# The MLP's input features in another order: weights loaded to match, four heads' worth of copies made whole, one pair of heads moved by DMA

## The chip, the cores and the metric

The kernel runs on one core of a Trainium2 chip. Its engines are TensorE (PE: matmuls, with weight loads PEld), VectorE (DVE), ScalarE (ACT), GpSimd (POOL) and SyncE (SP, which issues DMAs). The metric is the device time of one execution in microseconds. Before the change it is 640.87 us, the median of three runs (640.73 to 641.13).

## The reference

Two stages. The first is a delta-rule recurrence over 768 tokens for 4 batches and 8 heads of size 48; its output, with the heads side by side, is the input of an MLP with 384 inputs, 2048 hidden units and SiLU.

```python
B, H, S, D = q.shape                      # 4, 8, 768, 48
k_n = k / (norm(k) + 1e-6)
for t in range(S):
    y[t] = q[t] @ state
    state = state + beta[t] * outer(k_n[t], v[t] - k_n[t] @ state)
x = y.transpose(0, 2, 1, 3).reshape(B * S, H * D)   # 3072 x 384
h = x @ w_in                              # 384 x 2048
out = (h / (1 + exp(-h))) @ w_out         # 2048 x 384
```

The weights arrive as 64-bit floating point numbers. The kernel reads them as pairs of 32-bit words and makes fp32 of them itself.

## The kernel before

**Attention.** The 768 tokens are six chunks of 128, a chunk c is two halves hf of 64. Inside a chunk the recurrence is solved as a triangular system: scores of keys with keys, an inverse of blocks of 32x32 (`invert`, on VectorE: for each m one L628 and one L633), a merge of blocks (`merge`, L783; for the first chunk `merge_half`, L807), then `keys`, `inner`, `update` of the state, and the outputs: `old` (L909, queries with the state) and `new` (L922, scores with the new values), both into a PSUM bank pyc. The four batches are two groups g of two. Heads come in NP = 4 pairs p with members e. In pyc a head (p, e) takes the 48 rows from 64 * (1 - e) and the columns of p: the odd heads are at rows 0 to 47, the even ones at rows 64 to 111.

**From attention to the MLP.** A half-chunk's MLP input is the tile xT: 128 partitions, NKT = 3 tiles of 128 features, 256 tokens (64 of each batch). Feature f = 48 * head + d is at partition f % 128 of tile f // 128, so heads cross partitions and tiles. `even_heads` copies the odd heads' 48 rows of pyc into the tile part in one copy (48x512), and the even heads into xT in six copies of 48, 32 or 16 rows. Both are by ScalarE (L545) or, once, by VectorE (L548). The odd heads then go from part to xT by DMA, five for a half-chunk, issued by SP in `move` (L902). Matmuls of the first MLP layer (`hidden`, L1049, into the PSUM tile phid) read xT; ScalarE's SiLU is L1059. For the first half of chunk 0 there is no state yet, and `first_outputs` (L887) multiplies straight from a copy of the new values in the tile slab (which lies in sums_of_w) into two banks, one for even and one for odd heads; xT is the first (L545) with the second added (L896).

**Weights.** w_in is fetched in eight pieces of 256 columns, each by three DMAs of 128 partitions (`fetch_w_in`, L292), into whatever room is free then: tiles named raw, w_out or sums_of_g in the profile. `narrow` turns a piece into fp32 in steps: two activations on ScalarE (L232, L233), two operations on VectorE (L237, L241), one on GpSimd (L245). Pieces 0 to 7 are narrowed in order. w_out follows in eight pieces (L306).

**What sets the order.** Every engine's instructions are pinned to the order in which the code emits them. Around the change it is written out by hand, in a string of letters (`script`): r runs half a step of the MLP, f and b push a weight piece on (f its next step, b its beginning), i a step of `invert` of chunk 1, p a step of `prepare(1)`, s one of `solve`. All of SP's DMAs are one line (`in_line`), issued in order. Where `deep` is set, a DMA also waits until the one two places before it in the line has landed. That is so for the loads of q of chunk 1 and for fetches 3, 6 and 5; fetches 0, 1, 2 and 4 are issued without it. Their order on SP is: k and q of chunk 0; fetches 0 and 1; k of chunk 1; v of chunk 0; fetch 2; q of chunk 1; fetches 4, 3, 6 and 5; fetch 7. Then, around 95 us, `block_in` (L583) reads the 32x32 blocks of chunk 1 back from DRAM into g, the factors that `invert` starts from, and the first `move` follows it.

For chunk 1, `invert` ends in `put_up`: two block transposes (L606 into xe_y, which the merges read as a moving operand, and L608 into up) and copies.

Of the kernel before, what the change touches and what calls it, by code (L numbers as in the profile page):

```python
# [19 lines left out]
def kernel(  # L20
# [13 lines left out]
    P = 128  # L34
# [236 lines left out]
    SLAB = B * NP * 2 * D + D  # L271
# [10 lines left out]
    def fetch_w_in(i):  # L282
# [7 lines left out]
        src = moe_w_in.rearrange("(a p) f -> p a f", p=P)[:, :, i * WF : (i + 1) * WF].bitcast(U32)  # L290
        for a in range(NKT):
            in_line(nc.sync.dma_start(out=raw[:, a], in_=src[:, a]))  # L292
# [309 lines left out]
    def put_up(x):  # L602

        both = work.tile([P, BH, T], FP32, name="xe_y", tag="g", bufs=1)
        xes[1], ys[1] = both[:], both[:].rearrange("p (g h) t -> p g h t", g=2)
        pin(nc.vector.transpose(out=both[:].rearrange("p n s -> p s n"), in_=x))  # L606
# [229 lines left out]
    def inner(c, g, hf, room=CC):  # L836
# [9 lines left out]
        if c == 0 and hf == 0:  # L846
            by = (by_act, by_dve) if g == 0 else (by_dve, by_act)
            at = slab[:, g * HB * NP * 2 * D + D :][:, 0 : HB * NP * 2 * D]
# [27 lines left out]
    def first_outputs(g):  # L876

        pys = [bank(A, f"py{e}") for e in range(2)]
        for u in range(HB):
            for a in range(NKT):  # L880
                for n in range(2):
                    for half in range(2):
                        f = P * a + W * half
                        h = f // D + n
                        p, e = h // 2, h % 2
                        at = ((g * HB + u) * NP + p) * 2 * D + D + f - D * h
                        pin(nc.tensor.matmul(  # L887
                            pys[e][HALVES[half], C * a + W * u : C * a + W * (u + 1)],
                            lhsT=slab[on(e, 0, g), at : at + W], rhs=aps[0, g][1][on(e, 0, g), u, h, :],
                            start=True, stop=True,  # L890
                        ))
        xT, half = x_half(0, g, 0)
        to = xT[:, :, half]
        even, odd = (py[:, 0 : NKT * C].rearrange("p (a t) -> p a t", a=NKT) for py in pys)
        by_act(to, even)
        pin(nc.vector.tensor_tensor(out=to, in0=to, in1=odd, op=ALU.add))  # L896
# [20 lines left out]
    def new(c, g, hf):  # L917
# [8 lines left out]
        copies.append(even_heads(c, g, hf, py))  # L926
# [4 lines left out]
    def even_heads(c, g, hf, py):  # L931

        xT, half = x_half(c, g, hf)
        if g == 0:
            parts[c, hf] = work.tile([P, 2, NP, C], FP32, name="part", tag="x", bufs=1)
        part = parts[c, hf][:, g]
        by = by_dve if c == 1 and hf == 0 and g == 1 else by_act
        by(part[0:D], py[0:D].rearrange("p (a t) -> p a t", a=NP))
        if c == 0:
            yield  # L940
        for h in chained(range(1, H, 2), range(0, H, 2)):
            if c > 0 and h == 0:
                yield
            f = D * h
            while f < D * (h + 1):
                n, at = min(D * (h + 1) - f, P - f % P), W * (1 - h % 2) + f - D * h
                while h % 2 == 0 and (n > T and at % W or f % P % W and n > T):
                    n = T
                to = xT[f % P : f % P + n, f // P, half]
                if h % 2 == 1:  # L950
                    if g == 1:
                        moves.append((
                            xT[f % P : f % P + n, f // P].rearrange("p (g t) -> p g t", g=2),
                            parts[c, hf][at : at + n, :, h // 2, :],
                        ))
                else:
                    by(to, py[at : at + n, C * (h // 2) : C * (h // 2 + 1)])
# [655 lines left out]
```

## Time and profile before

| | |
|---|---|
| median of three runs | 640.87 us |
| profiled execution | 646.08 us, its span 644.3 us |
| granted TensorE clock, mean | 0.973 |
| TensorE busy | 623.5 us, 97% |
| VectorE, ScalarE, GpSimd busy | 401.2, 217.2, 94.3 us |
| moved by DMA | 53.69 MB |

The profile is of one execution of its own, longer than the timed ones. It gives each instruction by engine and line of the kernel, with its output and inputs (out<-in), and, behind a number in brackets or a bar, the idle time of the engine before it and what ended that. A row of the view by stage gives the stretch, its length, busy time and number of instructions of PE, PEld, DVE, ACT and POOL, then the granted TensorE clock, the share of time in which the DMA engines were busy, and GB/s. A row of waits gives who waited, for whom, the sum in us, how often, and the longest. The chain of waits is followed back from the last instruction; a row has its start, its length and what it was. In the timeline a row has start, length, engine, line and instruction; SPq is the issuing of a DMA by SP, waits included where rows are merged. A row of DMA issues ends with KB each and the median us from issue to landing. Rows by tile give minimum, median and maximum in ns.

### The profile page before, as it was taken

How to read it: one execution, taken by the hardware profiler on the slowest of the kernel's cores; microseconds unless marked ns; L12 is line 12 of the kernel's file. 1: busy time of each engine (PE TensorE's matmuls, PEld its weight loads, DVE VectorE, ACT ScalarE, POOL GpSimd, SP SyncE). 2: the span in 40 equal slices, each digit the busy share in tenths (PEclk: the TensorE clock that was granted, in tenths of full speed). 3: DMA queues.
4: the chain of work that ended last, by engine and by line, in shares of the span. 5: the costliest groups of instructions: out<-in, count | busy, mean ns of one | idle time of the engine just before them, and what ended most of it. 6: DMA issues, size and time to landing. Idle time of an engine off the chain costs nothing.

```text
span 644.3 us, 21893 instructions
## 1 busy us (share of the span) xinstructions
PE 623.5 (97%) x9642; PEld 550.1 (85%) x9642; DVE 401.2 (62%) x917; ACT 217.2 (34%) x512; POOL 94.3 (15%) x96
## 2 busy tenths in 40 slices
PE   6879999999999999999999999999999999999997
PEld 4677787756789988999989989989989989889997
DVE  5845688988865986563987563987464974212112
ACT  2655656151342122451122451122451122441120
POOL 5332630237011020010020010020001000000000
PEclk9759799999999999999999999999999999999999
DMA  9755445170278433268434268334173033100101
GB/s 190 164 141 163 146 97 132 50 148 3 58 150 145 62 85 50 54 133 136 70 79 55 47 137 138 69 79 56 26 154 76 9 79 48 40 14 1 25 0 25
DMA packets 141695, 53.69 MB, mean 83 GB/s; under 512 B 113296, under 2 KB 135056, under 8 KB 141600
## 3 DMA queue, kind: packets, MB, share of 16 engines
q1 hardware_dynamic: 141264, 52.14, 40.2%
q8 instruction: 76, 1.25, 0.8%
q10 hardware_dynamic: 336, 0.15, 0.1%
q14 instruction: 19, 0.16, 0.1%
HBM read 39.62 MB, written 10.49 MB: 78 GB/s over the span
## 4 chain that ended last, share of the span: by engine, by line
PE 92%; DMA 2%; issue 2%; DVE 1%; ACT 1%; SPq 1%; POOL 0%; DVEq 0%; POOLq 0%
PE phid L1049 39%; PE px L1156 16%; PE py L1156 12%; PE po L1084 7%; PE pa L530 3%; PE pz L841 2%; PE ph L829 2%; PE pyc L922 2%; PE pu L861 2%; PE pyc L909 2%; PE pt L501 1%; DMA kb<-in_k_dram 1%; DMA xT<-part 1%; PE px L783 1%; PE py L783 1%
## 5 line engine op out<-in xcount | busy, mean ns | idle before, releaser
L1049 PE MATMUL phid<-xT,w_in 128*128 128x256 f32 x1152 | 259.6, 383 | 2.5 <-DMA xT<-part 1.5
L1049 PEld LDWEIGHTS phid<-xT,w_in 128*128 128x128 f32 x1152 | 217.2, 191 | 33.6 <-issue 4.1
L1059 ACT ACTIVATE gT<-phid 128x512 f32<-128x512 f32 x88 | 52.6, 598 | 147.1 <-PE phid L1049 138.5
L628 DVE SCALAR_TENSOR_TENSOR rank<-g,step,x 128x31 f32<-128x31 f32 (+15 forms) x124 | 49.7, 401 | 36.9 <-DMA g<-blocks 33.4
L1138 DVE TENSOR_TENSOR sums_of_g<-gT 128x384 f32<-128x384 f32 (+1 forms) x60 | 29.8, 516 | 56.5 <-ACT gT L1059 46.0
L1156 PE MATMUL py<-w_out,sums_of_g 128*128 128x192 f32 x320 | 56.8, 329 | 0.0
L1156 PE MATMUL px<-sums_of_w,sums_of_g 128*128 128x192 f32 x320 | 56.6, 329 | 0.0
L1156 PEld LDWEIGHTS px<-sums_of_w,sums_of_g 128*128 128x128 f32 x320 | 52.2, 190 | 0.5
L1156 PEld LDWEIGHTS py<-w_out,sums_of_g 128*128 128x128 f32 x320 | 52.2, 190 | 0.4
L633 DVE TENSOR_TENSOR x<-x,rank 128x31 f32<-128x31 f32 (+15 forms) x124 | 42.5, 343 | 4.3
L468 POOL TENSOR_TENSOR vf<-vf,n_slot 128x768 f32<-128x768 f32 x10 | 14.9, 1490 | 167.9 <-DMA vf<-in_v_dram 121.8
L868 DVE TENSOR_TENSOR state<-state,pu 48x384 f32<-48x384 f32 x44 | 24.3, 552 | 21.9 <-PE pu L861 20.9
L545 ACT COPY xT<-pyc 48x128 f32<-48x128 f32 (+2 forms) x126 | 32.7, 260 | 1.7
L489 DVE STREAM_TRANSPOSE kq<-stage 128x512 f32<-128x512 f32 x28 | 28.2, 1112 | 3.9 <-DMA stage<-in_q_dram 3.8
L1156 PE MATMUL px<-sums_of_w,gT 128*128 128x192 f32 x160 | 28.4, 329 | 0.0
L1156 PE MATMUL py<-w_out,gT 128*128 128x192 f32 x160 | 28.4, 329 | 0.0
L1156 PE MATMUL px<-w_out,gT 128*128 128x192 f32 x160 | 28.0, 327 | 0.0
L841 PEld LDWEIGHTS pz<-vf,xi 64*64 64x64 f32 x768 | 25.2, 142 | 3.2 <-issue 2.6
L551 POOL COPY g<-x 64x256 f32<-64x256 f32 x4 | 5.0, 1242 | 152.5 <-DVE x L636 152.5
L1156 PEld LDWEIGHTS px<-w_out,gT 128*128 128x128 f32 x160 | 26.4, 190 | 0.6
L841 PE MATMUL pz<-vf,xi 64*64 64x48 f32 x768 | 26.9, 226 | 0.0
L1156 PEld LDWEIGHTS py<-w_out,gT 128*128 128x128 f32 x160 | 26.1, 190 | 0.3
(197 smaller groups left out, 831.1 us busy)
## 6 DMA issues: line engine op xcount, KB each, us to landing
vf<-in_v_dram SPq DMA_DIRECT2D x48, 96.0 KB, 3.1
out_dram<-o SPq DMA_DIRECT2D x42, 96.0 KB, 2.2
w_out<-in_moe_w_in_dram SPq DMA_DIRECT2D x12, 256.0 KB, 3.5
sums_of_w<-in_moe_w_out_dram SPq DMA_DIRECT2D x8, 384.0 KB, 4.4
blocks<-ap SPq DMA_DIRECT2D x40, 64.0 KB, 1.9
g<-blocks SPq DMA_DIRECT2D x5, 512.0 KB, 3.7
kb<-in_k_dram SPq DMA_DIRECT2D x12, 192.0 KB, 4.4
kb<-in_k_dram SPq DMA_DIRECT2D x24, 96.0 KB, 4.5
```

The lines of the kernel that those rows point to most:

```text
L489: pin(nc.vector.transpose(out=kqs[c, b][:, :, j, :].rearrange("p a (i m) -> p a m i", i=T), in_=src.rearrange("p a (m d) -> p a m d", d=D) ...
L530: pin(nc.tensor.matmul(pa[e][half, p * n * W : (p + 1) * n * W], lhsT=kq[rows, p, 0, half], rhs=kq[rows, p, js[0] : js[-1] + 1, half], sta ...
L545: return pin(nc.scalar.copy(to, of))
L628: pin(nc.vector.scalar_tensor_tensor(out=tv, in0=g[:, 0:m, m : m + 1].to_broadcast([P, m, n]), scalar=step[:, m : m + 1], in1=x[:, m : m + ...
L633: yield pin(nc.vector.tensor_tensor(out=x[:, 0:m, m:T], in0=x[:, 0:m, m:T], in1=tv, op=ALU.add))
L841: yield pin(nc.tensor.matmul(pz[rows, n * D : (n + 1) * D], lhsT=xis[g][rows, u * H + 2 * p + e, :], rhs=vfs[c][rows, hf, g * HB + u, p, : ...
L868: pin(nc.vector.tensor_tensor(out=to, in0=to, in1=by_heads(pu[of]), op=ALU.add))
L1049: pin(nc.tensor.matmul(ph[:, j * GT : (j + 1) * GT], lhsT=w_in[:, a, (2 * f + j) * P : (2 * f + j + 1) * P], rhs=xTs[c, hf][:, a, :], star ...
L1059: pin(nc.scalar.activation(out=hidden_of(c, hf, f), in_=ph[:], func=ACTF.Silu, scale=-0.5 if in_blocks(c) else 0.5))
L1084: pin(nc.tensor.matmul(pos[i][:, 0:DM], lhsT=hidden_of(0, hf, f // 2)[:, at : at + C], rhs=w_outs[f // HFF][:, f % HFF, :], start=(f == 0) ...
L1138: pin(nc.vector.tensor_tensor(out=sums_of_g[:, k, fs], in0=of[0], in1=of[1], op=op))
L1156: pin(nc.tensor.matmul(to, lhsT=at, rhs=quarter(f, *b) if isinstance(b, tuple) else sums_of_w[b][:, f], start=start and f == 0, stop=f == ...
```

## The change

**Feature order.** The features of xT are laid out as pyc has them. Tile a holds pair a whole: its odd head at partitions 0 to 47, its even head at 64 to 111. The last pair, p = 3, is cut into three times 16 rows, which fill partitions 48 to 63 (odd head) and 112 to 127 (even head) of the three tiles. Rows of w_in are put in the same order by their loads: a fetch is now four DMAs, for each member e one of 48 partitions with three rows each and one of 16 partitions with three rows each.

**Copies.** `rows_out` takes the place of `even_heads`: for each g two copies of the last pair into part (48x128) and two copies of three pairs into xT (48x384), so eight for a half-chunk in place of fourteen. Six DMAs of 16 partitions move the last pair from part to xT, in place of five.

**Order on SP and ScalarE.** For the second half of chunk 0, `move` and then `block_in(1)` come directly after `new`, before `copy_out`; `block_in(1)` is gone from `prepare`. In the script one f step (on ScalarE the beginning of a weight piece) moves behind two r steps. TensorE's order is unchanged.

**First outputs.** Both heads that share a slice of 64 features are accumulated in one bank; the addition goes, and ScalarE and VectorE copy half each. The slab has a stride of 416 per batch, the last pair's pieces apart, filled by two copies for each g; it is 1664 elements long in place of 1584.

**put_up.** The transpose L606 writes its output without a stride, and the merges of chunk 1 read it with one of 32 elements.

```diff
@@ setup
-    SLAB = B * NP * 2 * D + D
+    E = D // NKT
+    LAST = NKT * W + 2 * D - W
+    SPAN = LAST + NKT * W
+    SLAB = B * SPAN
@@ fetch_w_in
-        src = moe_w_in.rearrange("(a p) f -> p a f", p=P)[:, :, i * WF : (i + 1) * WF].bitcast(U32)
-        for a in range(NKT):
-            in_line(nc.sync.dma_start(out=raw[:, a], in_=src[:, a]))
+        cols = slice(i * WF, (i + 1) * WF)
+        whole = moe_w_in[0 : 2 * D * NKT].rearrange("(a e d) f -> e d a f", a=NKT, e=2)[:, :, :, cols].bitcast(U32)
+        split = moe_w_in[2 * D * NKT : DM].rearrange("(e a i) f -> e i a f", a=NKT, e=2)[:, :, :, cols].bitcast(U32)
+        for e in range(2):
+            at = W * (1 - e)
+            in_line(nc.sync.dma_start(out=raw[at : at + D], in_=whole[e]))
+            in_line(nc.sync.dma_start(out=raw[at + D : at + W], in_=split[e]))
@@ put_up
-        xes[1], ys[1] = both[:], both[:].rearrange("p (g h) t -> p g h t", g=2)
-        pin(nc.vector.transpose(out=both[:].rearrange("p n s -> p s n"), in_=x))
+        turned = both[:].rearrange("p n t -> p (n t)").rearrange("p (s n) -> p s n", s=T)
+        xes[1], ys[1] = turned.rearrange("p s n -> p n s"), both[:].rearrange("p (g h) t -> p g h t", g=2)
+        pin(nc.vector.transpose(out=turned, in_=x))
@@ inner, for chunk 0, half 0
-            by[0](at.rearrange("p (n w) -> p n w", w=2 * D)[:, :, 0:D], pz[:, 0:DM].rearrange("p (n d) -> p n d", d=D))
-            by[1](to, by_heads(pz))
+            by[0](at[:, :, 0 : NKT * W].rearrange("p u (a w) -> p u a w", a=NKT)[:, :, :, 0:D], of[:, :, 0:NKT])
+            by[1](
+                at[:, :, LAST:SPAN].rearrange("p u (a w) -> p u a w", a=NKT)[:, :, :, 0:E],
+                of[:, :, NKT].rearrange("p u (a i) -> p u a i", a=NKT),
+            )
+            by[1](to, of)
@@ first_outputs
-        by_act(to, even)
-        pin(nc.vector.tensor_tensor(out=to, in0=to, in1=odd, op=ALU.add))
+        for u, by in enumerate((by_act, by_dve)):
+            cols = slice(W * u, W * (u + 1))
+            by(xT[:, 0:NKT, half][:, :, cols], py[:, 0 : NKT * C].rearrange("p (a t) -> p a t", a=NKT)[:, :, cols])
@@ even_heads becomes rows_out
+        of = py[:].rearrange("p (a t) -> p a t", a=NP)
+        for at in (0, W):
+            by(part[at : at + D, half], of[at : at + D, NKT])
+            if g == 1:
+                for a in range(NKT):
+                    moves.append((xT[at + D : at + W, a], part[at + E * a : at + E * (a + 1)]))
+        yield
+        for at in (0, W):
+            by(xT[at : at + D, :, half], of[at : at + D, 0:NKT])
         yield
@@ solve, chunk 0
             together(new(0, 0, 1), new(0, 1, 1))
+            move()
+            block_in(1)
             copy_out()
             copy_out()
-            move()
@@ prepare
-        block_in(1)
@@ script
-... i p i p f r i r i2 r ...
+... i p i p r2 f i i2 r ...
```

More of the change, by code (lines that the diff above doesn't have):

```diff
@@ L876, in first_outputs @@
     def first_outputs(g):
-        pys = [bank(A, f"py{e}") for e in range(2)]
+        py = bank(A, "py")
         for u in range(HB):
@@ L925, in new, with rows_out @@
             ))
[L926 removed]
+        copies.append(rows_out(c, g, hf, py))
         go(copies[-1])
     copies = []
[L931 removed]
+    def rows_out(c, g, hf, py):
         xT, half = x_half(c, g, hf)
         if g == 0:
[L935 to L936 removed]
+            parts[c, hf] = work.tile([P, GT], FP32, name="part", tag="x", bufs=1)
+        part = parts[c, hf]
         by = by_dve if c == 1 and hf == 0 and g == 1 else by_act
[L938 to L957, printed above, removed]
[L958 removed]
+        of = py[:].rearrange("p (a t) -> p a t", a=NP)
[7 more added lines that the diff above has]
+            by(xT[at : at + D, :, half], of[at : at + D, 0:NKT])
         yield
```

22 lines of the change are left out of this document (9 added, 13 removed).

## The prediction

> **What bounds the kernel now.** I read the page's head first, then the busy time by stage, then who TensorE waits for, then the chain of waits, and last the sync engine's queue (SP, which issues nearly all DMAs).
>
> ```profile
> span 644.3 us, 21893 instructions
> PE 623.5 (97%) x9642; PEld 550.1 (85%) x9642; DVE 401.2 (62%) x917; ACT 217.2 (34%) x512; POOL 94.3 (15%) x96
> ```
> ```profile
> 0.00:53.00 53.00, 41.43 (x1254) 34.81 (x1255) 34.24 (x90) 25.45 (x64) 21.48 (x34) 0.74 0.75 163
> 53.00:80.00 27.00, 24.25 (x558) 19.59 (x557) 16.48 (x29) 16.82 (x29) 12.32 (x10) 0.87 0.52 159
> 80.00:102.00 22.00, 20.67 (x594) 17.00 (x591) 17.76 (x52) 14.27 (x34) 6.66 (x6) 1.00 0.45 106
> 223.00:320.00 97.00, 96.67 (x1448) 88.97 (x1447) 64.30 (x155) 29.30 (x76) 8.49 (x9) 1.00 0.49 87
> 510.00:562.00 52.00, 51.80 (x943) 46.88 (x944) 28.52 (x63) 14.78 (x37) 1.24 (x1) 1.00 0.26 49
> ```
> TensorE is busy in 623.5 of 644.3 us. From 223 us on its idle time is some 0.3 us per hundred, so copies saved there on ScalarE or VectorE buy nothing. What can move lies before 102 us: 11.6 us idle in the first row, 2.75 in the second, 1.33 in the third. The column behind the busy times is the granted clock (0.74, 0.87, 1.00).
>
> ```profile
> PE px L807 <- issue: 1.6, 1, 1.6
> PE phid L1049 <- DMA xT<-part: 1.5, 2, 1.3
> ```
> ```profile
> 92.55 1.04 ACT part L545 x2
> ...
> 95.25 1.45 SPq L902
> ...
> 98.70 2.70 DMA xT<-part
> ...
> 101.54 20.09 PE phid L1049 x92
> ```
> Of TensorE's waits only the second touches the code that changes: the first half-chunk whose odd heads go by DMA (pieces of part into xT). In the chain, ScalarE copies part, SP issues five moves, the last lands 2.70 us later, and TensorE, idle for 1.33 us, goes on at 101.54. The other 0.2 us of this wait fall at 560 us.
>
> The sum is made against the profiled execution: 646.08 us, 5.2 above the median of 640.87; differences are carried over as they are.
>
> **The change part by part.** TensorE's instructions stay the same in number and order.
>
> Copies and moves of a half-chunk. Before, two copies of part and twelve small copies into xT; after, four small ones of part (48x128) and four of 48x384.
>
> ```profile
> L545 ACT COPY part<-pyc 48x512 f32<-48x512 f32 x21 | 11.2, 578 | 22.8 <-PE pyc L922 18.5 <-DMA stage<-in_q_dram 4.3
> L545 ACT COPY xT<-pyc 48x128 f32<-48x128 f32 x42 | 11.0, 262 | 0.8
> L902 SPq DMA_DIRECT2D xT<-part x55: 597/612/1519, 95.2 to 570.5; - x55
> ```
> ```profile
> 94.78 0.34 SPq L583 DMA_DIRECT2D g<-blocks  x1
> 95.17 4.13 SPq L902 DMA_DIRECT2D xT<-part  x5
> ```
> Four part copies at 0.27 us take 1.08, as the two did (1.04). In the first half-chunk the moves no longer stand behind the read of g, so the first can be issued when the third copy is done: 92.55 + 0.81 = 93.4. Six issues at 0.65 (0.612 and its gap) instead of five put the last at 96.65; landing after 2.0 to 2.7 us, it is there at 98.7 to 99.4. TensorE came to its wait at 101.54 - 1.33 = 100.21, so that wait goes: **-1.33 us**. What is late next there is ScalarE, which read two raw weight pieces in that place; the script's moved f step puts the first activation between them. In all later half-chunks the sixth issue costs SP 0.65 us and nobody waits; at 560 us it may undo or double the 0.2 us.
>
> The read of g moves behind the six moves: from 94.78 to about 97.3, 2.5 us later. VectorE's inversion starts with it.
>
> ```profile
> 98.72 0.27 DVE L628 SCALAR_TENSOR_TENSOR rank<-g,step,sums_of_w 128x31 f32<-128x31 f32 x1 [1.38 <-ACT gT L1059]
> ...
> 135.25 2.04 DVE L606 STREAM_TRANSPOSE xe_y<-sums_of_w 128x1024 f32<-128x1024 f32 x1
> ```
> ```profile
> 141.29 1.22 PE py L783 x82
> ```
> ```profile
> L1301 DVE STREAM_TRANSPOSE sums_of_w<-blocks x1: 1250/1250/1250, 15.3 to 15.3; 128x1024 f32<-128x1024 f32 x1
> ```
> xe_y is ready at 137.29, TensorE wants it at 141.29: 4.0 us of cover. 2.5 are used by the later read and 1.33 by TensorE coming earlier; the transpose, which now writes without a stride, should fall from 2.04 towards the 1.25 of L1301, which leaves 0.9. Cost: nothing; if g lands later still, TensorE pays what exceeds 0.9.
>
> The merges of that chunk now read xe_y with a stride of 32 elements. No row shows TensorE reading so: between 0 and a doubling of the 1.22 us of L783; I take 0, since these 32x32 products overlap one another.
> [...]
>
> First outputs and slab. One bank with accumulation replaces two banks and an addition; the slab copy is split in two. ScalarE and VectorE lose some 0.5 us twice, while TensorE has other work in its order; it doesn't wait for either. The slab's memset grows by 5%. Cost 0.
>
> Weight loads. Each of the eight fetches of w_in is now four DMAs in place of three: 48 partitions (288 KB) and 16 (96 KB), once per half. Fetches 3, 6 and 5 are paced: a load waits until the one two places before it has landed, and SP waits with it, with everything behind it on its queue.
>
> ```profile
> 9.88 4.09 SPq L292 DMA_DIRECT2D raw<-in_moe_w_in_dram  x6
> ...
> 26.60 1.59 SPq L292 DMA_DIRECT2D w_out<-in_moe_w_in_dram  x3
> 31.54 8.01 SPq L142 DMA_DIRECT2D sums_of_g<-in_q_dram  x6
> 39.60 7.46 SPq L292 DMA_DIRECT2D w_out<-in_moe_w_in_dram  x6
> 48.30 4.17 SPq L292 DMA_DIRECT2D raw<-in_moe_w_in_dram  x3
> 52.92 4.86 SPq L292 DMA_DIRECT2D w_out<-in_moe_w_in_dram  x3
> 57.87 2.64 SPq L292 DMA_DIRECT2D sums_of_g<-in_moe_w_in_dram  x3
> ```
> ```profile
> 56.73 0.90 ACT L232 ACTIVATE w_in<-w_out 128x768 f32<-128x768 f32 x1
> ...
> 66.40 0.89 ACT L232 ACTIVATE w_in<-w_out 128x768 f32<-128x768 f32 x1
> ```
> ```profile
> 68.33 0.28 PE L807 MATMUL px<-xi,xe_y 32*32 32x32 f32 x6 [1.59 <-issue]
> ```
> ScalarE asks for piece 3 at 56.73 and for piece 5 at 66.40. Behind piece 5 on ScalarE stand the copies that TensorE's px waits for (the idle 1.59 us before 68.33), so there each us of lateness is a us of the end.
> A paced fetch of three took 4.62 and 4.95 us from start to start, which is 1.5 landings L: L = 3.2. With four loads it takes 2 L. Fetch 4's third load is issued about 1.5 us after 39.60 and lands at about 45; from it fetches 3, 6 and 5 are six landings, and the last small load is there 0.4 later. Piece 5 is ready at 45.4 + s + 6 L, where s is how much later fetch 4 begins.
>
> ```profile
> w_out<-in_moe_w_in_dram SPq DMA_DIRECT2D x12, 256.0 KB, 3.5
> ...
> stage<-in_q_dram SPq DMA_DIRECT2D x8, 176.0 KB, 3.5
> stage<-in_q_dram SPq DMA_DIRECT2D x16, 88.0 KB, 4.5
> ```
> Bounds of L: 3.2 as now, if fewer partitions cost nothing; 4.5 as for the 16-partition halves of stage, which land a us later than the 32-partition ones with twice the bytes. Taken: 3.8, the middle. Bounds of s: 0.7 (the q loads wait for fetch 2's third load instead of its second) and 4 (the six large loads of fetches 0 to 2 hold the queues 0.6 longer each, and four more issues of 0.68 don't hide). Taken: 2.3.
> So piece 5 is ready at 45.4 + 2.3 + 22.8 = 70.5, **4.1 us late**; bounds 65.3 (1.1 early) and 76.4 (10.0 late). Piece 3, four landings earlier, is ready at 55.3 (bounds 52.5 and 58.4): late only at the far end.
> [...]
>
> Sum: +4.1 - 1.33 = +2.8: 648.9 us profiled, **643.6 us** against the median.
>
> **The rivals.**
> The loads stay hidden (the other side): L at or below 3.3 and s near 0.7 keep piece 5 ahead of 66.40. For it: DMAs are busy only for 0.52 of the time in the row from 53 us, so the pacing is latency, not bandwidth. Against: the stage rows. It decides where 6 L + s falls under 21.0. Then the 1.33 remain: 639.5.
> The halves collide hard: L = 4.5, s = 4: 10.0 late, and TensorE, idle so long, is granted half its clock again. The 0.87 of the row 53 to 80 is 27 x 0.13 x 2 = 7 us at half clock; as much again would cost 3.5, half of it 1.7. 640.87 + 10.0 - 1.33 + 1.7 = 651.2.
> The change doesn't do what it says: the loads are hidden, but at 100.2 TensorE stops for another reason (a bank of hidden held by ScalarE's weight piece, or the later g eats the 0.9): 640.9.
>
> **How the numbers follow.** Forecast 0.47 (own range 641.8 to 648); hidden 0.25; collision 0.17; no gain 0.11. A measurement of this kernel tells about 0.2%, 1.3 us, from no change. Faster takes the hidden case, 0.25; same takes the third and the forecast's lower edge, 0.13; slower the rest, 0.62. The range runs from the hidden case with a little more (the strided write and 560 us), 638.9, to the collision, 651.0, which leaves about 0.12 out.
>
> **What would show it.** Right: ScalarE's wait before L232 of piece 5 is put down to the DMA of w_in, px's idle time before it grows from 1.59 to 5 or more, SP's stretches of the paced fetches grow from under 5 to above 7 us, the wait for xT from part is gone, and g's read stands behind the moves. Wrong: no wait for w_in on ScalarE, stretches of 6.5 us or less and TensorE through 100 us without a stop: then it is 639.5. The step most likely wrong is L.

## The result, and the profile after

The changed kernel takes **656.81 us** (median; 656.48 to 660.61), the kernel before, beside it, 641.0 (640.73 to 642.21): ratio **1.0256** (95% interval 1.0216 to 1.0296). The forecast was 643.6 us with a range of 638.9 to 651.0, so the direction was right and the size was not. The profiled execution of the changed kernel is its slowest (660.61 us); what sets it apart is named below.

Page of the changed kernel: the head and TensorE's busy time.

```profile
span 658.8 us, 21875 instructions
PE 627.0 (95%) x9642; PEld 553.6 (84%) x9642; DVE 399.7 (61%) x915; ACT 203.2 (31%) x450; POOL 94.1 (14%) x96
```

The span grew by 14.5 us over the profile before (644.3). TensorE's busy time grew by 3.5 of it, its idle time by 11.0 (from 20.8 to 31.8). ScalarE has 14 us less work, as the change means to, and that buys nothing.

Busy time by stage of the changed kernel (start:end, length, then PE, PEld, DVE, ACT and POOL busy, the granted clock, the DMA share and GB/s).

```profile
0.00:53.00 53.00, 39.50 (x1186) 33.09 (x1187) 32.91 (x90) 24.09 (x63) 20.86 (x34) 0.74 0.84 139
53.00:80.00 27.00, 16.84 (x468) 13.52 (x466) 10.89 (x20) 9.50 (x17) 6.22 (x4) 0.91 0.49 107
80.00:102.00 22.00, 19.67 (x456) 16.23 (x457) 15.06 (x39) 13.58 (x28) 9.61 (x9) 0.80 0.60 157
```

Against the rows before: TensorE does 1.9 us less in the first 53 us and 7.4 us less in the next 27. In the first row the DMAs are busy longer (0.84 of the time against 0.75) and move less (139 GB/s against 163). That is not latency: the same bytes take more of the DMA engines' time.

Waits of ScalarE and of TensorE in the changed kernel (line waited for: us in all, times, longest).

```profile
ACT w_in L232 <- DMA w_out<-in_moe_w_in_dram: 14.5, 2, 9.9
PE px L815 <- ACT xe_y L552: 10.1, 1, 10.1
```

ScalarE, in order of time.

```profile
63.09 0.90 ACT L232 ACTIVATE w_in<-w_out 128x768 f32<-128x768 f32 x1 [4.51 <-DMA w_out<-in_moe_w_in_dram]
...
79.36 0.89 ACT L232 ACTIVATE w_in<-w_out 128x768 f32<-128x768 f32 x1 [9.95 <-DMA w_out<-in_moe_w_in_dram]
...
81.14 0.74 ACT L552 COPY xi<-pl 32x256 f32<-32x256 f32 x2
81.91 0.36 ACT L552 COPY xe_y<-py 32x256 f32<-32x256 f32 x1
```

This is the wait that the prediction named, in its place: the narrowing of piece 5 waits for its load, and the copies that TensorE's px needs stand behind it. Piece 5 is read at 79.36 where it was asked for at 66.40 before: 12.96 us late, not 4.1. Piece 3, which the forecast had in time, is 6.4 late (63.09 against 56.73).

SP's queue shows where the 13 us come from (start, length of the issue).

```profile
31.58 0.63 SPq L298 DMA_DIRECT2D w_out<-in_moe_w_in_dram  x1
...
38.29 7.56 SPq L142 DMA_DIRECT2D sums_of_g<-in_q_dram  x6
45.90 0.88 SPq L298 DMA_DIRECT2D w_out<-in_moe_w_in_dram  x1
...
47.31 0.42 SPq L298 DMA_DIRECT2D w_out<-in_moe_w_in_dram  x1
...
53.52 0.31 SPq L298 DMA_DIRECT2D w_out<-in_moe_w_in_dram  x1
...
58.42 0.31 SPq L298 DMA_DIRECT2D w_out<-in_moe_w_in_dram  x1
...
74.80 0.31 SPq L298 DMA_DIRECT2D w_out<-in_moe_w_in_dram  x1
```

Fetch 4 starts at 45.90 where it started at 39.60: s = 6.3. Its third load, issued at 47.31, frees fetch 3 at 53.52: 6.2 us. From there to 79.3, when piece 5 is complete, are 25.8 us, which hold six landings: L = 25.8/6 = 4.3.

Part of the rest is TensorE's clock. Finer stretches of the changed kernel around the stop, and of the one that this profiled execution has beside it:

```profile
72.00:75.00 3.00, 0.20 (x14) 0.09 (x6) 0.42 (x1) 0.00 (x0) 0.90 (x1) 1.00 0.53 118
75.00:82.00 7.00, 0.00 (x0) 0.00 (x0) 0.00 (x0) 2.59 (x5) 0.00 (x0) 0.52 0.90 167
82.00:89.00 7.00, 6.67 (x106) 5.71 (x107) 5.38 (x9) 4.89 (x8) 4.79 (x5) 0.50 0.60 181
89.00:96.00 7.00, 7.00 (x148) 5.48 (x148) 4.00 (x14) 2.47 (x6) 2.90 (x3) 1.00 0.53 165
255.00:263.00 8.00, 7.19 (x144) 6.80 (x144) 7.01 (x28) 1.16 (x2) 0.00 (x0) 0.58 0.80 90
```

Three us into the stop, which begins at 72.20, the granted clock falls to half (1.00 from 72 to 75 us, 0.52 from 75 to 82), and it stays there (0.50) for the first 6.67 us of work after it, which at full clock is work of 3.3 us. So long a stop is not needed for it: in the profile before the granted clock is 0.57 over the 8 us from 69 to 77 us behind a wait of only 1.59 us. The last row is a second stretch with a reduced clock, after two short waits at 254 us (0.93 and 0.75 us); the 0.42 of the clock that is missing there over 8 us is 3.4 us of work, about what the profiled execution stands above the median (3.8).

The reduced clock of the profile before is 3.4 us of work as well, so against that profile the half clock behind the stop costs nothing new. Against the median it does: the mean granted clock of that profiled execution is 0.973, while 15 of the 19 executions of the kernel before that ran beside e1 have 0.978 to 0.981. In e1, which loads w_in into 128 partitions at a time, the clock is 1.00 from 53 to 89 us; the pages of e3, e17 and e18, which do so too, have nine tenths or more in every slice from 48 us on.

### The profile page after: what moved, and what is told of

Same layout as the page of the kernel before. It is cut to its first block, busy times and chain, and to the rows that moved or that the text cites. A ratio compares the mean times of both kernels' runs of the same rounds, so it can differ in the third digit from the quotient of the medians.

```text
span 658.8 us, 21875 instructions
## 1 busy us (share of the span) xinstructions
PE 627.0 (95%) x9642; PEld 553.6 (84%) x9642; DVE 399.7 (61%) x915; ACT 203.2 (31%) x450; POOL 94.1 (14%) x96
## 4 chain that ended last, share of the span: by engine, by line
PE 80%; DMA 10%; DVE 5%; SPq 4%; issue 1%; ACT 1%; POOL 0%; DVEq 0%; POOLq 0%; ACTq 0%
PE phid L1048 34%; PE px L1155 15%; PE py L1155 11%; PE po L1083 6%; DMA w_out<-in_moe_w_in_dram 4%; PE pa L537 3%; DMA raw<-in_moe_w_in_dram 2%; PE pz L849 2%; PE ph L837 2%; DVE rank L636 2%; SPq L142 2%; DVE x L641 2%; PE pu L874 2%; PE pyc L932 2%; PE pyc L919 1%; PE py L791 1%
## 5 line engine op out<-in xcount | busy, mean ns | idle before, releaser
L881 DVE TENSOR_TENSOR state<-state,pu 48x384 f32<-48x384 f32 x44 | 24.3, 552 | 22.8 <-PE pu L874 21.8
L1155 PE MATMUL px<-w_out,gT 128*128 128x192 f32 x160 | 30.6, 348 | 0.0
L1155 PEld LDWEIGHTS px<-w_out,gT 128*128 128x128 f32 x160 | 28.9, 204 | 0.6
L1155 PEld LDWEIGHTS px<-sums_of_w,gT 128*128 128x128 f32 x160 | 26.1, 190 | 0.2
```

The lines of the kernel that those rows point to most:

```text
L881: pin(nc.vector.tensor_tensor(out=to, in0=to, in1=by_heads(pu[of]), op=ALU.add))
L1155: pin(nc.tensor.matmul(to, lhsT=at, rhs=quarter(f, *b) if isinstance(b, tuple) else sums_of_w[b][:, f], start=start and f == 0, stop=f == ...
```

## The experiments

Ratios are to the kernel before, run beside them, with 95% intervals; the median of the kernel before was 639.47, 640.42, 640.72, 641.80 and 641.20 us in the five sets. One such interval is 0.2 to 0.4% wide to each side (1.3 to 2.6 us), so effects of a us are read from the traces and the timing only bounds them.

### The loads alone, and all but the loads

```diff
 changed kernel, fetch_w_in (e1):
-            in_line(nc.sync.dma_start(out=raw[at : at + D], in_=whole[e]))
-            in_line(nc.sync.dma_start(out=raw[at + D : at + W], in_=split[e]))
+        for a in range(NKT):
+            in_line(nc.sync.dma_start(out=raw[:, a], in_=src[:, a]))
 kernel before, fetch_w_in (e2): the same lines the other way round
```

> The changed kernel with the loads of w_in as before (three loads of 128 partitions for each fetch); all else of the change stays. The weights' rows then stand in the old order while the features stand in the new one, so the MLP multiplies features with the wrong rows. If the loads are the whole loss, piece 5 is on time again, TensorE's idle time of 10.12 us at 72.20 us falls to about 1.6, and the time is that of my sum without its load term, 639.5 us (638.5 to 640.5). If a good part of the loss lies in the copies, the strided reads or the later read of g, the time stays above 643 us.

> The kernel before with only the four loads of 48 and 16 partitions for each fetch of w_in; features and copies as before, so the MLP multiplies features with the wrong rows. If the loads are the whole loss: 656 to 659 us (the changed kernel's 656.8 and the 1.33 us of the wait for part that is kept), with fetch 4 some 6 us late and paced landings of some 4.3 us. If the loss needs the rest of the change: under 646 us.

Measured: without the new loads 642.14 us, **1.0040** (1.0016 to 1.0064); with only the new loads 654.89 us, **1.0248** (1.0212 to 1.0285). The kernel before with the new loads:

```profile
ACT w_in L232 <- DMA w_out<-in_moe_w_in_dram: 13.7, 2, 10.5
```

So the loads are nearly the whole loss: they alone add 15.4 us to the kernel before (654.89 less 639.47), the whole change 15.8 (656.81 less 641.0). The changed kernel with the old loads, page:

```profile
span 638.7 us, 21856 instructions
PE 620.6 (97%) x9642; PEld 548.6 (86%) x9642; DVE 399.8 (63%) x915; ACT 203.2 (32%) x450; POOL 94.4 (15%) x96
```

Between this profile and the changed kernel's, whose code differs in the loads alone, idle time goes from 18.1 to 31.8 us (13.7) and busy time from 620.6 to 627.0 (6.4, about what the two stretches with a reduced clock hold). But the first run is a miss of another kind: it was to be 639.5, faster than before by 0.2%, and it is slower by 0.4%. That is taken up below.

### What makes the loads slow: their number, their order, or the partitions they reach

```diff
 kernel before, fetch_w_in (e3):
-        for a in range(NKT):
-            in_line(nc.sync.dma_start(out=raw[:, a], in_=src[:, a]))
+        for a, cols in ((0, slice(0, 2 * WF)), (1, slice(0, WF)), (2, slice(0, 2 * WF)), (1, slice(WF, 2 * WF))):
+            in_line(nc.sync.dma_start(out=raw[:, a, cols], in_=src[:, a, cols]))
 changed kernel, fetch_w_in (e4): both loads of whole[e] first, then both of split[e]
 kernel before, fetch_w_in (e5; e6 with rows = slice(k, P, 4)):
+        for k in range(4):
+            rows = slice(T * k, T * (k + 1))
+            in_line(nc.sync.dma_start(out=raw[rows], in_=src[rows]))
```

> The kernel before with four loads for each fetch that all go to 128 partitions: 256, 128, 256 and 128 KB (the middle one cut in two by columns). Same bytes and the same number of loads as the change, but every load reaches both halves. If the number of paced loads is what costs: each paced fetch takes two landings of 3.2 us, 6.4 in place of 4.8, piece 5 is 4 to 6 us late, 645 to 650 us. If it is that a load reaches 48 or 16 partitions of one half: the smaller loads land sooner, fetch 4 starts within 1 us of 39.60, piece 5 is at most 1.5 us late, 640.5 to 642.5 us.

> The changed kernel with the order of its four loads altered: both of 48 partitions first (one for each half), then both of 16, so that the two that are in flight go to opposite halves of the partitions. If two loads into the same half stand in each other's way, the pairs land sooner, the paced fetches fall from 8.5 to 7 us, fetch 4 starts 2 to 3 us sooner, and the time is 648 to 653 us. If each load is slow by itself, whatever flies beside it: 655 to 659 us.

> The kernel before with four loads for each fetch of w_in, each of 32 neighbouring partitions and 192 KB, with pieces of 2048 bytes as before. If a load is slow because it reaches a narrow range of partitions: packets take about twice as long as in the wide loads, fetch 4 starts 4 us or more late, and the time is 650 to 662 us. If it was the small share of 16 partitions alone, or the uneven sizes, that made the change slow: 640 to 645 us.

> As the kernel with 32 neighbouring partitions for each load, but each load takes every fourth partition: the same number of loads, partitions, packets and bytes, spread over all 128. If the range of partitions that a load reaches is the cause: 639.5 to 643 us, as with the four loads of 128 partitions, and packets as short as there. If the number of partitions of a load is the cause, wherever they lie: as slow as the loads of neighbouring partitions.

Measured: four wide loads 640.93 us, **1.0018** (0.9994 to 1.0042); halves in turn 654.54 us, **1.0244** (1.0204 to 1.0284); 32 neighbouring partitions 649.38 us, **1.0129** (1.0093 to 1.0165); 32 spread partitions 652.19 us, **1.0181** (1.0144 to 1.0217).

The number of loads is not the cause. With four wide ones fetch 4 does start late, at 42.31 in place of 39.60 (1 us was expected), but ScalarE waits only 1.03 us for piece 5, and TensorE's stop ahead of px is 1.46 us where it was 1.59. The order hardly is: the changed kernel's 1.0256 and 1.0244 overlap, though ScalarE's two waits fell from 14.5 to 4.6 us in the profiled execution, the fastest of its four. The last pair decides, by its loads and not by its time (neighbouring partitions cost nearly what was expected of them, with piece 5 awaited for 4.9 us; the spread ones cost more, against the theory). DMA view from 9 to 24 us, where fetches 0 and 1 fly with nothing to pace them (packets, mean rate; issues, size, median us to landing). Before, then the changed kernel:

```profile
DMA packets 9082, 3.17 MB, mean 211 GB/s; under 512 B 8310, under 2 KB 8310, under 8 KB 9078
raw<-in_moe_w_in_dram SPq DMA_DIRECT2D x6, 256.0 KB, 5.2
```
```profile
DMA packets 5818, 2.55 MB, mean 170 GB/s; under 512 B 5046, under 2 KB 5046, under 8 KB 5814
raw<-in_moe_w_in_dram SPq DMA_DIRECT2D x4, 96.0 KB, 8.0
```

32 neighbouring partitions, then 32 spread:

```profile
DMA packets 6884, 2.75 MB, mean 184 GB/s; under 512 B 6112, under 2 KB 6112, under 8 KB 6880
raw<-in_moe_w_in_dram SPq DMA_DIRECT2D x8, 192.0 KB, 6.6
```
```profile
DMA packets 7805, 2.93 MB, mean 195 GB/s; under 512 B 7033, under 2 KB 7033, under 8 KB 7801
raw<-in_moe_w_in_dram SPq DMA_DIRECT2D x8, 192.0 KB, 3.6
```

The same loads by number, bytes, size of pieces and number of partitions: 6.6 us to land when the 32 partitions are neighbours, 3.6 when they are spread over all 128. The means over 15 us also hold the loads of q and k. Between 12.5 and 16 us the rates lie further apart: 354 GB/s before, 291 with four wide loads, 266 with 32 spread partitions, 217 with 32 neighbours and 184 in the changed kernel; from 16 to 24 us all five lie between 164 and 189. Fetch 2, behind k and v in SP's queue, is issued late in the same order: by 0.6 us with four wide loads, 1.7, 2.8 and 5.0. What counts is which partitions a load reaches. The changed kernel's loads of 96 KB into the 16 partitions from 48 or 112 on, with loads of 288 KB beside them, took 8.0 us to land. One rival is left: with the partitions, the rows of w_in in DRAM that a load reads are neighbours or spread too, and no run parts the two.

That the spread loads nevertheless lost 1.8% has another reason, in their trace (ScalarE in order of time, and the chain of waits):

```profile
53.25 0.89 ACT L232 ACTIVATE w_in<-w_out 128x768 f32<-128x768 f32 x1 [14.10 <-DMA w_out<-in_moe_w_in_dram]
```
```profile
49.64 0.60 SPq L293
...
50.34 2.85 DMA w_out<-in_moe_w_in_dram
```

This is piece 2, whose own loads were issued from 28.26 to 31.64 us; it waits for a load issued at about 50, which belongs to fetch 3, its neighbour in the same tile. The likely reason is that the program orders strided writes into one tile more coarsely than contiguous ones; that was not tested. So this kernel's time says nothing of the partitions, and a version of the change with fast loads was not made.

### How much of it is the pacing

```diff
 changed kernel (e11): for fetches 3, 6 and 5
-            behind(dma, pace.pop() if pace else line[-2], Sync)
+            behind(dma, pace.pop() if pace else line[-depth[-1]], Sync)
 ...
-        depth.append(True)
+        depth.append(4 if fetch is fetch_w_in else 2)
 e12: also, for chunk 2's writes of blocks
-    c == 0 and j % 2 == 1,
+    c in (0, 2) and j % 2 == 1,
```

> The changed kernel with its paced loads of w_in (fetches 3, 6 and 5) waiting for the load four places before in place of two; all else of the change. Fetch 4 starts as late as in the change (6.3 us), but then the 1920 KB up to piece 5 come at the rate that narrow loads have (some 200 GB/s in the full stretches) and not at two landings for each fetch. If the pacing by landings carries 6 or more of the 12.9 us: piece 5 is there at 63 to 69 us, at most 2.5 us late, and the time is 642 to 647 us. If the loads are limited by their rate, and the pacing only shares it out: 652 to 657 us.

> As the last, with chunk 2's writes of blocks on two queues as well. If the changed kernel's TensorE reaches the merges of chunk 2 before xe (it waited 1.7 us there in the changed kernel): 1 to 1.7 us less than without the second queue. If not: no difference.

Measured: 650.94 us, **1.0150** (1.0111 to 1.0188), and 653.73 us, 1.0177 (1.0138 to 1.0216). The first lies between its two expectations; the second was to be no slower than the first, and their intervals overlap. With four in flight:

```profile
49.28 1.32 SPq L298 DMA_DIRECT2D w_out<-in_moe_w_in_dram  x1
```
```profile
73.13 0.92 ACT L232 ACTIVATE w_in<-w_out 128x768 f32<-128x768 f32 x1 [2.15 <-issue]
```

Piece 5 is read at 73.13 in place of 79.36, though fetch 4 began still later (49.28 against 45.90). From the start of fetch 4 to piece 5 it is 23.9 us, with two in flight 33.5, and ScalarE no longer waits for piece 5's load. But 10.2 us of the loss of 15.8 are left: the pacing carries about a third of it. The late start is none of its making, and from 60 to 72 us the DMA engines are now busy for 0.91 of the time and move 163 GB/s, so there the loads are slow by their rate. The second queue did not help; why is below.

### Where the gain of 1.33 us went

The 1.33 us were TensorE's wait at 100 us for part. In the changed kernel and in its variant with the old loads no such wait is left, as forecast. Still that variant is slower than the kernel before. First the moves alone, then the strided xe_y:

```diff
 kernel before (e7), after new(0, *, 1); block_in(1) leaves prepare, the copies of the even heads come behind move():
+            move()
+            block_in(1)
             copy_out()
             copy_out()
-            move()
 changed kernel with the old loads (e8), put_up:
-        pin(nc.vector.transpose(out=turned, in_=x))
+        pin(nc.vector.transpose(out=both[:].rearrange("p n s -> p s n"), in_=x))
```

> The kernel before with the moves of the first half-chunk issued ahead of the copies of its even heads and of the read of g, all else as before (loads, layout, first outputs, strides). If the cover of 4.0 us before the merges holds: TensorE's wait of 1.3 us at 100 us goes and nothing takes its place, ratio 0.998 (0.996 to 1.000). If the later read of g reaches TensorE at the merges near 141 us, or ScalarE's copies stop it at 100 us: 0.999 to 1.003.

> The changed kernel with the loads of w_in as before (features and weights' rows don't match, so the MLP's products are others) and with xe_y written and read as before, without the strided reads. That kernel with strided reads took 1.004 of the kernel before, and its merges read xe_y in 2.0 us in place of 1.3. If the strided read costs TensorE's time: 0.7 us less, ratio 1.001 to 1.004, and the merges' line falls back to 1.3. If it overlaps other work: no difference in the time though the line falls.

Measured: 640.67 us, **1.0016** (0.9991 to 1.0041), and 642.34 us, **1.0037** (1.0011 to 1.0062). The moves alone gain nothing that can be measured. Waits of TensorE from 85 us on, moves first:

```profile
PE py L783 <- DMA xe<-low: 1.5, 2, 1.0
```

The wait at 100 us is gone, and 136 us later TensorE waits 1.5 us that it did not wait before, in the merges of chunk 2, for xe. xe ends a chain: blocks written, g read back, some 30 us of inversion on VectorE, low written, xe read. In the profile of the four wide loads, otherwise the kernel before, the first of the two reads of xe, issued at 235.37, lands 2.2 us later, at 237.56, and TensorE comes at 238.44: a cover of at most 0.9 us, since the second read is issued 0.3 us after the first and its landing is not in the trace. The head of the chain is SP's queue. Four wide loads, then moves first, then the change with the old loads:

```profile
175.92 4.58 SPq L160 DMA_DIRECT2D stage<-in_q_dram  x7
180.67 5.47 SPq L197 DMA_DIRECT2D vf<-in_v_dram  x8
186.24 3.86 SPq L902 DMA_DIRECT2D xT<-part  x5
190.20 4.26 SPq L104 DMA_DIRECT2D blocks<-ap  x8
195.98 0.34 SPq L583 DMA_DIRECT2D g<-blocks  x1
```
```profile
185.10 4.27 SPq L902 DMA_DIRECT2D xT<-part  x5
189.47 4.27 SPq L104 DMA_DIRECT2D blocks<-ap  x8
195.22 0.34 SPq L583 DMA_DIRECT2D g<-blocks  x1
```
```profile
185.23 4.55 SPq L908 DMA_DIRECT2D xT<-part  x6
```

SP issues almost without a pause from 176 to 194 us. With the moves first TensorE is at the merges at 236.0 us, 2.4 sooner, but g is read only 0.8 us sooner; and the sixth move of each half-chunk stands in this queue, ahead of the writes.

The strided read of xe_y is seen in the rows of TensorE, and so is a cost that the prediction left out (old loads, then the kernel before; merges, then first outputs):

```profile
L787 PE MATMUL py<-xe_y,ap 32*32 32x32 f32 x128 | 2.0, 228 | 0.0
L894 PE MATMUL py<-ap,sums_of_w 64*64 64x64 f32 x96 | 3.8, 240 | 0.0
```
```profile
L783 PE MATMUL py<-xe_y,ap 32*32 32x32 f32 x128 | 1.3, 193 | 0.0
L887 PE MATMUL py<-ap,sums_of_w 64*64 64x64 f32 x96 | 2.6, 268 | 0.0
```

0.7 us for the strided read and 1.2 us for the first outputs, both of TensorE's busy time. The second figure depends on the execution: the row has 3.4 us in the changed kernel's own profile and 4.4 in that of e8, so the cost is 0.8 to 1.8; it lies in a stretch (40 to 53 us) whose granted clock differs between the profiles (0.65 before, 0.69 in the changed kernel, 0.75 with the old loads). With xe_y as before (e8) the merges' row is back at 1.3, but the time did not change (1.0037 against 1.0040): in that profile TensorE waited 2.0 us for xe at the merges of chunk 2, so what it has ahead of them it loses there.

The chain was then made later by mistake, shorter by leaving work out, and shorter in SP's queue:

```diff
 e9: e7, and e10: the kernel before, with chunk 2's writes of blocks on two queues
-    c == 0 and j % 2 == 1,
+    c in (0, 2) and j % 2 == 1,
 e13: e7, e14: the kernel before, e16: e15, in invert
+            if c == 2 and m > T - 7:
+                yield
+                continue
 e15: the changed kernel with the old loads and the slab and first_outputs of the kernel before
 e17: e7, and e18: the kernel before, with move() of (1, 1) behind block_in(2)
```

> The kernel before with the moves of the first half-chunk issued first (as in the run that did this alone, ratio 1.0016) and, for chunk 2, half of the eight writes of blocks issued by ScalarE's queue in place of SP's. In that run TensorE's wait at 100 us was gone, but it waited 1.03 and 0.51 us at 236 us, in the merges of chunk 2, for xe, which comes at the end of a chain: blocks written, g read back, 29 us of inversion, low written, xe read. If the gain was taken back by this chain: its eight issues of 3.8 us shrink to some 2, xe is there 1 to 2 us sooner, the wait at 236 us goes, and the ratio is 0.9975 (0.995 to 0.999). If the loss was elsewhere: 1.000 to 1.003 as without it, or more, where ScalarE's issues hold up its copies.

> The kernel before with only chunk 2's writes of blocks on two queues. TensorE does not wait for xe there (xe lands 0.9 to 1.5 us ahead of the merges), so if the theory of the chain holds, a sooner xe buys nothing: ratio 1.000 (0.998 to 1.002). If the writes were a cost by themselves: under 0.998.

> The kernel before with the moves issued first (1.0016 by itself) and with six of the 31 steps of chunk 2's inversion left out (12 small VectorE instructions, some 3 us; chunk 2's result is then incomplete). The order on every other engine stays. If TensorE's gain at 100 us was given back to the chain of chunk 2, at whose end it waited 1.5 us: the wait at 236 us goes and the ratio is 0.998 (0.996 to 0.999). If the gain never existed, or is given back elsewhere: 1.000 to 1.003, as without it.

> The kernel before with only those six steps of chunk 2's inversion left out (chunk 2's result is then incomplete). TensorE does not wait at the end of that chain there: 1.000 (0.998 to 1.002). If under 0.998, the chain was a bound of the kernel before as well, and the run with both tells nothing of the move.

> The changed kernel with the loads of w_in, the slab and the first outputs as before, so that the first half-chunk and the weights keep the old order while the other half-chunks have the new one (the MLP's products are others). The same with the new first outputs took 1.004, and their 96 matmuls 3.8 us of TensorE in place of 2.6. If the first outputs are what the rest of the change costs: 1.3 us less, ratio 1.001 to 1.002, as with the moves alone. If it is the copies and moves of the other half-chunks: 1.004 as before.

> As the last, and with six steps of chunk 2's inversion left out (chunk 2's result is then incomplete). If loads, first outputs and the chain of chunk 2 are all that stood against the gain of 1.33 us at 100 us: ratio 0.998 (0.996 to 1.000), what the sum without its load term said. If something is still missing: over 1.001.

> The kernel before with the moves of the first half-chunk first (1.0016 by itself), and with the five moves of chunk 1's second half-chunk issued behind chunk 2's writes of blocks and read of g in place of ahead of them. In all runs so far SP issues without a pause from about 176 to 196 us (loads of q, loads of v, these moves in 3.3 to 4.5 us, eight writes, the read of g), and the merges of chunk 2 wait for what follows. If SP's queue is the head of that chain: g is read 2 to 4 us sooner, TensorE's wait for xe at 236 us goes, and the ratio is 0.998 (0.9955 to 0.9995), a version that does the whole computation. If ScalarE's and VectorE's copies of the blocks set the writes' time anyway, or the chain is not what takes the gain back: 1.000 to 1.003.

> The kernel before with only those five moves behind the read of g. With the shorter inversion alone the kernel took 0.9983 of the time before, so some of this is to be had without the moves first: 0.9985 (0.997 to 1.001). If it is below the run with both, the moves first are worth nothing even where the chain does not stand against them.

| kernel | us | ratio | 95% interval |
|---|---|---|---|
| moves first, two queues (e9) | 644.14 | 1.0057 | 1.0031 to 1.0083 |
| two queues alone (e10) | 644.75 | 1.0059 | 1.0039 to 1.0080 |
| moves first, short inversion (e13) | 639.96 | 0.9984 | 0.9959 to 1.0009 |
| short inversion alone (e14) | 640.44 | 0.9983 | 0.9963 to 1.0002 |
| old loads, old first outputs (e15) | 642.69 | 1.0031 | 1.0008 to 1.0053 |
| the same, short inversion (e16) | 640.67 | 0.9987 | 0.9968 to 1.0005 |
| moves first, (1, 1) late (e17) | 643.04 | 1.0045 | 1.0021 to 1.0068 |
| (1, 1) late alone (e18) | 644.73 | 1.0052 | 1.0025 to 1.0080 |

Both attempts to speed up the chain with all its work made it later, where e9, e17 and e18 were to be faster than the kernel before and e10 as fast. With two queues (e10), ScalarE's share of the writes went out from 188.45, but SP reached its own only at 195.32, and g is read 3 us later than with four wide loads; the profile has SP waiting 7.1 us for these writes among its loads of v.

With the moves behind the read of g (e18) the read starts sooner, but the inversion does not. SP's read of g, GpSimd's clearing of x and VectorE's first step, (1, 1) late alone, then four wide loads, then TensorE's wait in (1, 1) late alone:

```profile
194.17 0.34 SPq L583 DMA_DIRECT2D g<-blocks  x1
...
199.33 0.95 POOL L565 MEMSET x<- 128x1024 f32 x1 [10.43 <-DMA xT<-part]
...
200.52 0.27 DVE L628 SCALAR_TENSOR_TENSOR rank<-g,step,x 128x31 f32<-128x31 f32 x1 [8.74 <-POOL x L566]
```
```profile
191.61 0.95 POOL L565 MEMSET x<- 128x1024 f32 x1 [1.74 <-DMA xT<-part]
...
199.47 0.27 DVE L628 SCALAR_TENSOR_TENSOR rank<-g,step,x 128x31 f32<-128x31 f32 x1 [6.87 <-DMA g<-blocks]
```
```profile
PE py L783 <- DMA xe<-low: 1.7, 2, 1.2
```

The read of g lands 3.4 us after its issue, at about 197.6, sooner than with four wide loads. But the first step comes at 200.52 and not at 199.47, because it no longer waits for g: it waits for x, the tile that the inversion works in. GpSimd clears x, and it cannot begin before the moves out of part have landed, since in the code part and x take the same room (both have the tag "x", with one buffer). The trace of e17 has the same wait (9.31 us, to 201.07). So these two versions took the moves out of the way of one head of the chain and put them in the way of another, and SP's queue by itself was not tested.

A chain that starts 1 us later turns a cover of at most 0.9 us into a wait of 1.7 us. The ratio of 1.005 is 3.5 us, twice that wait, and the kept trace, of an execution of 641.19 us, does not show the rest. Part of it may be the clock. Of the executions in which TensorE waits 1.5 to 2.0 us for xe in these merges, the changed kernel's has a reduced clock behind that wait (0.58 over 8 us, 3.4 us of work) and that of e8 a mean granted clock of 0.975, where those of e7, e9, e10, e15, e17 and e18 have 0.978 to 0.981 (e9 and e10: 1.00 from 223 to 320 us). The mean is 0.976 or less in seven of the twelve executions of e18, in four of 23 of the kernel before beside it.

That the chain bounds TensorE there is shown by the waits for xe in e9, e10, e17 and e18 (1.7 to 1.8 us) and from the other side: six steps less of inversion take away the wait of 1.6 us in the kernel with the old loads and first outputs and make it 0.44% faster (1.0031 to 0.9987). The kernel before gets 0.17% faster, at the edge of its interval.

What is not shown is the gain itself. With the chain out of the way the moves first should have kept their 1.33 us (0.2%); the ratios 0.9984 and 0.9983 are equal, with intervals too wide to exclude that much. In the profiles TensorE ends the merges of chunk 2 at 239.54 us with the moves first and 240.04 without, half a us sooner; another 0.5 us goes at 136 us, where TensorE, with the moves first, waits for xe_y, which the later read of g delays. Whether the rest of the 1.33 us is there and too small to see is left open. The old first outputs give 1.0031 for 1.0040, in the right direction and within the error. No version with all the work beat the kernel before.

## Why the prediction was wrong

**Place and mechanism: right.** Of the five signs of the last part four came as written: ScalarE's wait before piece 5 is put down to the DMA of w_in, px's idle time grew from 1.59 to 10.12, the wait for xT from part is gone, and g's read stands behind the moves (105.30 and 109.97). The fifth, longer stretches of the paced fetches, holds from start to start: 9.3 us for fetch 3 and 7.7 for fetch 6 (53.52, 62.84, 70.51).

**s, the failing step.** "Taken: 2.3", bounds 0.7 and 4; measured 6.3. With four wide loads fetch 4 starts 2.7 us late (42.31), so for the number of loads the term was near; the other 3.6 us are those of narrow loads. I priced slow loads in the paced stretch by a landing time and let the unpaced fetches 0 to 2 lose 0.6 us for each of six large loads. No row stands behind the 0.6, which was an estimate. There the DMAs were already the bound (a busy share of 0.75 over 53 us, 1.06 by the profile's count from 9 to 24 us), and narrow loads cut their rate: from 9 to 24 us 170 GB/s, at a share of 1.21, in place of 211. Fetch 2 was issued 5.0 us late (31.58 against 26.60), and the q loads behind it lost another 1.3. The sum of 6.3 breaks the upper bound of the hard case.

**L: right within its bounds.** Taken 3.8, bounds 3.2 and 4.5, measured 4.3. The six landings and the last small load were to take 22.8 + 0.4 us and took 25.8: 2.6 more. The third load of fetch 4 was to land 5.4 us after the start of fetch 4 (45 less 39.6) and took 7.6 (53.52 less 45.90): 2.2 more. With the 4.0 of s these are 8.8 us: the 12.96 that were measured less the 4.1 of the forecast.

**A us late is a us of the end: incomplete for long stops.** Behind the stop of 10.12 us came 6.67 us of work at a clock of 0.50, and TensorE's busy time differs by 6.4 us between the two profiles that differ in the loads alone (3.4 of it in the stretch at 255 us, which the other executions, all 3.5 us shorter or more, probably lack), where the forecast had nothing and the collision rival 1.7. That rival had the mechanism (0.17); its s was too small and its clock too cheap, and at 651.2 it stood outside the range that was to end with it, 651.0. A second step failed beside it, "differences are carried over as they are": the profile that the sum starts from has 3.4 us of half clock at 69 us, which its median execution mostly lacks, so in the median the half clock behind the stop comes on top.

**-1.33 us: the wait went, the gain did not.** I followed g to 141 us and no further. "In all later half-chunks the sixth issue costs SP 0.65 us and nobody waits" is the sentence that failed: behind these moves stand chunk 2's writes of blocks, and the merges at 238 us wait for what follows, with a cover of at most 0.9 us that the prediction had not looked at.

**Read of g, 0: held** but for 0.5 and 0.6 us at 136 us in two profiles (e13, e8). **Strided read of xe_y, 0:** measured 0.7, inside the bounds (0 to 1.2), though the products do overlap (128 of 193 ns each in 1.3 us before, of 228 ns in 2.0 us with the stride). **First outputs, 0:** measured 0.8 to 1.8 us of TensorE. That its instructions are the same in number is true; that they run as before is not: in the code the old order spreads neighbouring matmuls over all four pairs of row and column halves, the new one over two, and with the old first outputs the row is back at 2.6. These also have two banks without accumulation, so that the order is the reason is likely, not shown. The two rows together, some 2 us, are more than the gain that they stand against.

## What to carry to other kernels

A load's price was here not in its bytes alone but in which partitions it reaches, and with them which rows of DRAM: loads into 48 or 16 neighbours of one half took the DMAs' rate from 9 to 24 us from 211 to 170 GB/s, whereas four wide loads in place of three cost the kernel nothing that its time shows (1.0018). Apply such a price first where the queue is full, and only then where it is paced, and add the reduced clock that can follow a stop (here 0.50 for 6.67 us of work behind 10.12 us). Before booking the end of a wait as a gain, follow every chain whose pace is set elsewhere (here SP's queue) to the next place where TensorE meets it, however far. And before moving a transfer back, ask what takes the room of its source next: here x had to wait for part.

## What the runs showed of the hardware

Two things that are easily missed. A load into every fourth partition was nearly as good as one into all (266 GB/s from 12.5 to 16 us, 291 with four wide loads, 217 with 32 neighbours): 192 KB into 32 such partitions landed in 3.6 us, into 32 neighbours in 6.6. And a wait of TensorE that is far shorter than a stop of 10 us can be followed by a reduced clock: behind 1.59 us came a granted clock of 0.57 for 8 us in the profile before, behind 1.7 us one of 0.58 for 8 us in the changed kernel; with four wide loads, behind 1.46 us, none came (nine tenths or more in every slice of the page from 48 us on), nor in e9 and e10 behind 1.8 and 1.7 us at the merges (1.00 from 223 to 320 us). What decides it is not shown.
